# A convolution and two feed-forward layers on one core: other SBUF addresses for the activation tiles, and one gather buffer instead of two

## The chip, the core and the metric

The kernel runs on one core of a Trainium2 chip. The metric is device time in microseconds (us) from the first to the last instruction of one execution. The engines are TensorE (PE; its weight loads are listed apart as PEld), VectorE (DVE), ScalarE (ACT), GpSimd (POOL) and SyncE (SP), whose queue issues nearly all DMAs. SBUF is the on-chip memory of 128 partitions. A tile lies at one byte address, the same in each of its partitions; PSUM is the memory that TensorE writes.

## What is computed

A dynamic convolution with 7 taps and softmax weights over 2 x 4096 tokens of width 192, then two feed-forward layers of width 2048, the first with a leaky ReLU, the second with an ELU.

```python
w = np.exp(weight_gen - max); w = w / (sum(w) + 1e-09)      # per token, head, 7 taps
out = np.einsum('bshk,bskhg->bshg', w, x_unf)               # x_unf: the 7 last tokens
h = x @ w_in;  g = np.maximum(0.01 * h, h);            x = g @ w_out
h = x @ w_in;  g = np.where(h > 0, h, exp(min(h, 0)) - 1);  out = g @ w_out
```

## The kernel before

The 8192 tokens are cut into 16 blocks of 512. Each block goes through layer 0 and layer 1; a layer has 8 units, each of 256 of the 2048 hidden columns, so there are 256 units in all. Blocks 0 and 1 of layer 0 run interleaved at the start, then the two layers take turns: (0, 2), (1, 0), (1, 1), (0, 3), (1, 2), and so on.

All matrices are split into a high and a low part of type float32r, and three of the four partial products are added up. The weights (`win`, `wout`) stay in SBUF. TensorE is used as two halves of 64 rows: `issue` (L830) emits one matmul for the rows 0 to 63 and one for the rows 64 to 127 in turn. Both of a pair stream 512 columns. In the steady state a round of unit s holds 19 such pairs: nine h matmuls of unit s for each half, and ten output matmuls of unit s-4 for each half. The lower half does its h matmuls first, the upper half its output matmuls first; so of the 19 pairs 18 hold one h matmul (moving operand `xt` or `yt`, stationary operand `win`) and one output matmul (moving `gh` or `gl`, stationary `wout`), and one pair holds two output matmuls.

After a round ACT makes `w` from the PSUM tile `h` (L752 or L755, in layer 1 also L759 and, on DVE, L763), then the high part `gh` (ACT, L769) and DVE the low part `gl` (L772). `gh` and `gl` have four buffers each, 4096 bytes per partition.

From block 2 on the input of layer 0 is made by `conv_block` on DVE, transposed in 32 x 32 squares, written to DRAM (`spread`, L551) and read back in another order by two `gather` steps into two `dup` tiles: `gather(0)` is one DMA (L556), `gather(1)` two (L559). `high(0)` and `high(1)` on ACT (L573) and `low(0)` and `low(1)` on DVE (L576) turn them into the one `xt` tile. The first matmul of the block's first round waits for all of these (`fresh` and `tasks` in the code).

A planner (`Plan.order`) sets the order of the instructions on all engines from costs written in the code, the keys and the number of buffers of each ring. With one buffer in a ring, a step that takes it is put behind the last user of the tile before. Tiles are placed in SBUF one after another in the order of their creation: `ident`, `spare`, the weights, and then the rings. `new` (L186) hands a ring's tile out.

Of the kernel before, what the change touches and what calls it, by code (L numbers as in the profile page):

```python
# [8 lines left out]
F32 = mybir.dt.float32  # L9
# [11 lines left out]
P = 128  # L21
# [10 lines left out]
N = BS * P  # L32
# [30 lines left out]
WARM = 14  # L63

FILL = 0.5

HEAD = 30.0

# [97 lines left out]
def conv_moe_kernel(ctx: ExitStack, tc: tile.TileContext, x, wg, wi0, wi1, wo, out):  # L166
# [5 lines left out]
        "xt": (1, [P, 4, N], F32R), "yt": (2, [P, 4, N], F32R),  # L172
        "h": (2, [P, 2, N], F32), "w": (3, [P, 2 * N], F32),
        "gh": (4, [P, 2 * N], F32R), "gl": (4, [P, 2 * N], F32R),
        "dup": (2, [P, N], F32), "c": (1, [P, N], F32), "o": (1, [P, N], F32),
        "raw": (4, [P, 2 * 512 + 2], I32), "t": (2, [P, 512], I32),
    }
    const = ctx.enter_context(tc.tile_pool(name="const", bufs=1))
# [10 lines left out]
    def new(slot):  # L189
        bufs, shape, dt = rings[slot.ring]  # L190
        if slot.ring == "xs":

            if slot.ring not in lasting:
                lasting["xs"] = (sb.tile([P, 2 * shape[1], D], dt, name="xs"), [0])
            tile, n = lasting["xs"]
            r = n[0] % 2 * shape[1]
            slot.tile = tile[:, r : r + shape[1], :]
            n[0] += 1
            return slot.tile
        if bufs == 1 or slot.ring in ("h", "t"):  # L200

            tiles, n = lasting.setdefault(slot.ring, ([], [0]))
            if len(tiles) < bufs:
                pool = {"h": ps, "st": small, "e": small}.get(slot.ring, sb)
                tiles.append(pool.tile(shape, dt, name=f"{slot.ring}{len(tiles)}"))
            slot.tile = tiles[n[0] % bufs]
            n[0] += 1
            return slot.tile
        pool = small if slot.ring in ("ws", "raw") else sb
        slot.tile = pool.tile(shape, slot.dtype or dt, tag=slot.ring, name=slot.ring, bufs=bufs)  # L210
        return slot.tile

    ident = const.tile([P, P], F32, name="ident")
    spare = const.tile([P, 1], F32, name="spare")
    win = {}
    wout = {}
    for l in range(2):
# [29 lines left out]
    def split(src, hi_out, lo_out, key, names):  # L247
# [19 lines left out]
        def load():  # L267
            nc.sync.dma_start(new(raw).bitcast(U16)[:, 1 : 4 * n + 1], src.bitcast(U16))  # L268
# [5 lines left out]
        def leading():  # L274
            middle, top = parts()
            d = new(t)[:, :n].bitcast(F16).rearrange("p (n t) -> p n t", t=2)
            nc.scalar.activation(d[:, :, 1], top, AF.Copy)  # L277
# [51 lines left out]
    def conv_block(i, due):  # L329
# [8 lines left out]
        def load_w():  # L338
            n = BS * H * K
            dst = new(ws).rearrange("p a k -> p (a k)")  # L340
            nc.sync.dma_start(dst, wg[:, i * n : (i + 1) * n])  # L341
# [615 lines left out]
    with tc.manual_schedule():  # L957
# [8 lines left out]
        def turn(bank, count):  # L966
            for n in range(count):
                nc.tensor.matmul(bank[:, N // 2 : N // 2 + P], plain, plain, start=True, stop=True)  # L968
# [9 lines left out]
        for t in order:  # L978
            t.ins = t.emit()
            if t is plan.read_once:  # L980
                spare_bank = acc[1][0]
            turn(spare_bank, int(FILL * gaps.get(t, 0.0) / 0.27))

# [43 lines left out]
```

## Time and profile before

| what | value |
|---|---|
| median of 2 timed runs | 1130.34 us (1129.93 to 1130.75) |
| the profiled execution | 1129.36 us, of which the trace spans 1127.5 us |
| PE busy | 1120.0 us, 99% of the span, 9936 matmul records |
| DVE busy | 782.2 us, 69% |
| ACT busy | 788.5 us, 70% |
| granted TensorE clock | 1.0 in all 40 slices |
| chain that ended last | PE 98% |

The trace can be read by groups of equal instructions, by tile, in order of time and by stretches of time. Durations are of one profiled execution. The ends of matmuls are modelled and overlap with the next start, so the pace of TensorE is read from starts.

### The profile page before, as it was taken

How to read it: one execution, taken by the hardware profiler on the slowest of the kernel's cores; microseconds unless marked ns; L12 is line 12 of the kernel's file. 1: busy time of each engine (PE TensorE's matmuls, PEld its weight loads, DVE VectorE, ACT ScalarE, POOL GpSimd, SP SyncE). 2: the span in 40 equal slices, each digit the busy share in tenths (PEclk: the TensorE clock that was granted, in tenths of full speed). 3: DMA queues.
4: the chain of work that ended last, by engine and by line, in shares of the span. 5: the costliest groups of instructions: out<-in, count | busy, mean ns of one | idle time of the engine just before them, and what ended most of it. 6: DMA issues, size and time to landing. Idle time of an engine off the chain costs nothing.

```text
span 1127.5 us, 23936 instructions
## 1 busy us (share of the span) xinstructions
PE 1120.0 (99%) x9936; PEld 924.7 (82%) x9936; DVE 782.2 (69%) x969; ACT 788.5 (70%) x1011; POOL 11.7 (1%) x19
## 2 busy tenths in 40 slices
PE   8999999999999999999999999999999999999998
PEld 7888888888888888888888888888888888888886
DVE  7877989889899898998974463544636445363565
ACT  7989987575766757658576585756757566575675
POOL 4000000000000000000000000000000000000000
PEclk9999999999999999999999999999999999999999
DMA  6453120222203122030110000000010000000001
GB/s 222 142 159 94 44 73 15 87 73 68 73 1 99 43 68 73 17 122 3 29 34 16 20 1 15 20 16 20 1 34 1 15 20 1 15 1 15 1 1 29
DMA packets 28812, 50.23 MB, mean 45 GB/s; under 512 B 3104, under 2 KB 16288, under 8 KB 28704
## 3 DMA queue, kind: packets, MB, share of 16 engines
q1 hardware_dynamic: 28560, 48.57, 13.9%
q8 instruction: 78, 1.28, 0.5%
q14 instruction: 30, 0.25, 0.1%
q10 hardware_dynamic: 144, 0.13, 0.0%
HBM read 36.90 MB, written 11.80 MB: 43 GB/s over the span
## 4 chain that ended last, share of the span: by engine, by line
PE 98%; DMA 1%; DVE 0%; SPq 0%; issue 0%; ACT 0%; DVEq 0%
PE acc L830 51%; PE h L830 46%; DMA raw<-wi_in 1%; DVE gl L471 0%; PE h L489 0%; SPq L352 0%; DVE yt L457 0%; SPq L341 0%; SPq L268 0%; PE acc L968 0%; ACT raw L272 0%; DVE o L641 0%; DVE st L372 0%; ACT win L284 0%; DVE acc L387 0%
## 5 line engine op out<-in xcount | busy, mean ns | idle before, releaser
L830 PE MATMUL acc<-gh,wout 64*128 64x512 f32 (+1 forms) x3048 | 973.3, 386 | 0.0
L830 PE MATMUL acc<-gl,wout 64*128 64x512 f32 (+1 forms) x2032 | 784.4, 386 | 0.0
L830 PEld LDWEIGHTS acc<-gh,wout 64*128 64x128 f32 (+1 forms) x3048 | 560.9, 184 | 60.2
L830 PE MATMUL h<-yt,win 64*128 64x512 f32 (+1 forms) x2568 | 606.1, 387 | 0.9 <-ACT yt L453 0.9
L830 PEld LDWEIGHTS h<-yt,win 64*128 64x128 f32 (+1 forms) x2568 | 469.8, 184 | 54.1 <-ACT yt L453 1.1
L830 PE MATMUL h<-xt,win 64*128 64x512 f32 x2016 | 476.7, 386 | 0.0
L772 DVE TENSOR_TENSOR gl<-w,gh 128x1024 fp32r<-128x1024 f32 (+1 forms) x257 | 312.4, 1220 | 168.7 <-ACT gh L769 167.7
L830 PEld LDWEIGHTS acc<-gl,wout 64*128 64x128 f32 (+1 forms) x2032 | 374.0, 184 | 40.6 <-issue 0.4
L830 PEld LDWEIGHTS h<-xt,win 64*128 64x128 f32 x2016 | 371.0, 184 | 39.6
L769 ACT ACTIVATE gh<-w 128x1024 fp32r<-128x1024 f32 (+1 forms) x257 | 267.9, 1049 | 3.0
L752 ACT ACTIVATE w<-h 128x1024 f32<-128x1024 f32 x128 | 131.4, 1027 | 193.2 <-PE h L830 190.8
L763 DVE SCALAR_TENSOR_TENSOR w<-w,h 128x512 f32<-128x512 f32 x256 | 164.4, 684 | 127.6 <-ACT w L759 126.5
L755 ACT ACTIVATE w<-h 128x1024 f32<-128x1024 f32 x129 | 131.5, 1020 | 117.2 <-PE h L830 116.5
L759 ACT ACTIVATE w<-w 128x512 f32<-128x512 f32 x256 | 147.5, 624 | 4.0
L428 DVE TENSOR_TENSOR a<-a,prod 128x768 f32<-128x768 f32 x84 | 80.2, 955 | 1.6
L420 DVE TENSOR_TENSOR prod<-xs,ws 128x768 f32<-128x768 f32 x84 | 80.2, 954 | 1.3
L600 DVE TENSOR_TENSOR c<-acc,c 128x512 f32<-128x512 f32 (+1 forms) x32 | 22.0, 687 | 32.6 <-ACT o L649 26.0
L593 ACT ACTIVATE c<-acc 64x512 f32<-64x512 f32 x32 | 19.1, 595 | 4.6 <-PE acc L830 3.8
L272 ACT ACTIVATE raw<-raw 128x384 int32<-128x384 uint32 (+3 forms) x30 | 17.1, 572 | 5.2 <-DMA raw<-wi_in 5.2
L277 ACT ACTIVATE t<-raw 128x384 f16<-128x384 bf16 (+3 forms) x30 | 19.9, 664 | 0.0
L576 DVE TENSOR_TENSOR xt<-dup,xt 128x512 fp32r<-128x512 f32 x28 | 18.0, 686 | 0.0
L281 DVE CUSTOM_DVE_ANT_0 raw<-raw,t 128x768 uint16<-128x768 uint16 (+1 forms) x26 | 15.4, 606 | 1.7 <-ACT t L277 1.7
(56 smaller groups left out, 238.5 us busy)
## 6 DMA issues: line engine op xcount, KB each, us to landing
xs<-x_in SPq DMA_DIRECT2D x14, 960.0 KB, 5.0
raw<-wo_in SPq DMA_DIRECT2D x16, 384.0 KB, 3.5
scratch<-prod SPq DMA_DIRECT2D x56, 96.0 KB, 3.2
raw<-wi_in SPq DMA_DIRECT2D x10, 512.0 KB, 4.2
out_t<-o SPq DMA_DIRECT2D x15, 256.0 KB, 2.6
dup<-scratch SPq DMA_DIRECT2D x14, 256.0 KB, 3.0
dup<-scratch SPq DMA_DIRECT2D x28, 128.0 KB, 2.9
out_t<-c SPq DMA_DIRECT2D x16, 128.0 KB, 2.5
```

The lines of the kernel that those rows point to most:

```text
L277: nc.scalar.activation(d[:, :, 1], top, AF.Copy)
L420: nc.vector.tensor_tensor(out=prods() if k else sums(), in0=rows_of(k, BS + k).rearrange("p s (h g) -> p (s h) g", g=G), in1=scaled(k).to_ ...
L428: nc.vector.tensor_tensor(out=sums(), in0=sums(), in1=prods(), op=ALU.add)
L593: nc.scalar.activation(new(c)[0:64], B[64:P], AF.Copy)
L600: nc.vector.tensor_tensor(out=c.tile[0:n], in0=B[0:n], in1=c.tile[0:n], op=ALU.add)
L752: nc.scalar.activation(cols(w), flat(), AF.Prelu, alpha=0.01)
L755: nc.scalar.activation(cols(w), flat(), AF.Relu, scale=-1.0)
L759: nc.scalar.activation(c, c, AF.Exp, scale=-1.0)
L763: nc.vector.scalar_tensor_tensor(out=c, in0=c, scalar=1.0, in1=h.tile[:, j, :], op0=ALU.subtract, op1=ALU.max,)
L769: nc.scalar.activation(cols(gh), cols(w), AF.Copy)
L772: return nc.vector.tensor_tensor(out=cols(gl), in0=cols(w), in1=cols(gh).bitcast(F32), op=ALU.subtract).ins
L830: i = nc.tensor.matmul(out_ap, w, x_ap, start=start, stop=stop).ins
```

## The change

Four things: the base of nearly all tiles moves up by 32 bytes, since `spare` grows from 4 to 36 bytes and places are given out in steps of 32; each `gh` and `gl` tile gets 16 more columns (64 bytes) behind the 1024 that are used; the ring `dup` has one buffer; and `spare` is filled over 9 columns instead of 1.

```diff
+SHIFT = 16
...
-        "dup": (2, [P, N], F32), "c": (1, [P, N], F32), "o": (1, [P, N], F32),
+        "dup": (1, [P, N], F32), "c": (1, [P, N], F32), "o": (1, [P, N], F32),
...
         pool = small if slot.ring in ("ws", "raw") else sb
+        n = shape[-1]
+        if slot.ring in ("gh", "gl"):
+            shape = [P, n + SHIFT]
         slot.tile = pool.tile(shape, slot.dtype or dt, tag=slot.ring, name=slot.ring, bufs=bufs)
+        if slot.ring in ("gh", "gl"):
+            slot.tile = slot.tile[:, :n]
         return slot.tile
 
     ident = const.tile([P, P], F32, name="ident")
-    spare = const.tile([P, 1], F32, name="spare")
+    spare = const.tile([P, 9], F32, name="spare")
```

The addresses in the two built programs, modulo 512 bytes:

| tiles | before | change |
|---|---|---|
| `ident` | 128 | 128 |
| `win`, `wout`, `xt`, `yt`, `w`, `dup`, `c`, `o` | 160 | 192 |
| `gl`, four buffers | 160 each | 192, 256, 320, 384 |
| `gh`, four buffers | 160 each | 448, 0, 64, 128 |

The slices that matmuls read of `win`, `wout`, `xt` and `yt` start at multiples of 512 bytes within their tiles, those of `gh` and `gl` at multiples of 1024, so the operands have the remainders of the table. In front of the change every moving and every stationary operand of the 64-row matmuls lies at 160.

The order of TensorE's instructions is the same in both programs, row for row. On SP, ACT and DVE the steps of `gather(1)` move. SP at the first block that goes through `dup` (block 2), before (`raw` are weights on their way in, `dup` the gathered block):

```order
L551 DMA scratch<-prod 32x6x128 x4
L268 DMA raw<-wi_in 128x2048
L556 DMA dup<-scratch 128x512
L559 DMA dup<-scratch 64x512 x2
L268 DMA raw<-wi_in 128x2048
L268 DMA raw<-wo_in 128x1536
```

and with the change:

```order
L558 DMA scratch<-prod 32x6x128 x4
L275 DMA raw<-wi_in 128x2048
L563 DMA dup_1115<-scratch 128x512
L275 DMA raw<-wi_in 128x2048
L275 DMA raw<-wo_in 128x1536
L566 DMA dup_1115<-scratch 64x512 x2
```

The two DMAs of `gather(1)` stand behind one load of `wi` and one of `wo`. ACT at the same place, before (`w<-h` and `gh<-w` are two steps of one unit, the other rows weights):

```order
L272 ACTIVATE raw<-raw 128x512
L573 ACTIVATE xt_1176<-dup 128x512 x2
L752 ACTIVATE w<-h_323 128x1024
L769 ACTIVATE gh<-w 128x1024
L277 ACTIVATE t_96<-raw 128x512
L284 ACTIVATE win_76<-raw 128x512
L272 ACTIVATE raw<-raw 128x512
L752 ACTIVATE w<-h_286 128x1024
```

and with the change:

```order
L279 ACTIVATE raw<-raw 128x512
L580 ACTIVATE xt_1173<-dup_1115 128x512
L284 ACTIVATE t_96<-raw 128x512
L759 ACTIVATE w<-h_323 128x1024
L776 ACTIVATE gh<-w 128x1024
L291 ACTIVATE win_76<-raw 128x512
L291 ACTIVATE win_77<-raw 128x512
L279 ACTIVATE raw<-raw 128x512
L580 ACTIVATE xt_1173<-dup_1115 128x512
L759 ACTIVATE w<-h_286 128x1024
```

`high(1)` is now one unit later than `high(0)`, and the next `w<-h` stands behind it. DVE's `low(1)` moves in the same way, behind the next `gl`. In the later blocks the same pair of steps is torn apart by one or two units.

## Rows read from the trace of the kernel before

**Rows 1.** The page: busy time, TensorE's clock in 40 slices, chain that ended last.

```profile
PE 1120.0 (99%) x9936; PEld 924.7 (82%) x9936; DVE 782.2 (69%) x969; ACT 788.5 (70%) x1011; POOL 11.7 (1%) x19
...
PEclk9999999999999999999999999999999999999999
...
PE 98%; DMA 1%; DVE 0%; SPq 0%; issue 0%; ACT 0%; DVEq 0%
```

**Rows 2.** Groups by shape, PE: xcount | busy us, mean ns | idle before.

```profile
L830 PE MATMUL acc<-gh,wout 64*128 64x512 f32 x3024 | 965.7, 386 | 0.0
L830 PE MATMUL acc<-gl,wout 64*128 64x512 f32 x2016 | 778.3, 386 | 0.0
L830 PE MATMUL h<-yt,win 64*128 64x512 f32 x2544 | 599.7, 386 | 0.0
L830 PE MATMUL h<-xt,win 64*128 64x512 f32 x2016 | 476.7, 386 | 0.0
```

**Rows 3.** Order of time, PE, 500 us: start us, us, instruction, xcount.

```profile
500.15 0.39 PE L830 MATMUL acc<-gl,wout 64*128 64x512 f32 x1
500.16 0.39 PE L830 MATMUL h<-yt,win 64*128 64x512 f32 x1
500.38 0.39 PE L830 MATMUL acc<-gh,wout 64*128 64x512 f32 x1
...
504.46 0.39 PE L830 MATMUL acc<-gl,wout 64*128 64x512 f32 x1
504.46 0.39 PE L830 MATMUL h<-yt,win 64*128 64x512 f32 x1
```

**Rows 4.** Order of time, PE, the last unit: 512 columns, then 256.

```profile
1118.97 0.39 PE L830 MATMUL acc<-gh,wout 128*128 128x512 f32 x1
1119.20 0.39 PE L830 MATMUL acc<-gl,wout 128*128 128x512 f32 x1
...
1122.18 0.28 PE L830 MATMUL h<-gl,wout 128*128 128x256 f32 x1
1122.30 0.40 PE L830 MATMUL h<-gh,wout 128*128 128x256 f32 x2
1122.54 0.28 PE L830 MATMUL h<-gl,wout 128*128 128x256 f32 x1
```

**Rows 5.** Order of time, PE, the warm-up matmuls on `ident`; then by tile: min/median/max ns.

```profile
5.21 1.28 PE L968 MATMUL acc<-ident 128*128 128x128 f32 x10
...
L968 PE MATMUL acc<-ident x42: 271/275/582, 1.4 to 20.8; 128*128 128x128 f32 x42
```

**Rows 6.** Three stretches: length, busy us (x) of each engine, PEclk, DMA.

```profile
100.00:400.00 300.00, 300.00 (x2650) 247.82 (x2648) 269.96 (x343) 220.21 (x288) 0.00 (x0) 1.00 0.20 59
400.00:800.00 400.00, 400.00 (x3532) 330.65 (x3530) 273.02 (x322) 267.76 (x330) 0.00 (x0) 1.00 0.11 32
800.00:1000.00 200.00, 200.00 (x1768) 165.29 (x1766) 95.42 (x108) 132.31 (x162) 0.00 (x0) 1.00 0.04 12
```

**Rows 7.** Order of time, block 2's way into `xt`: SP, ACT, DVE, PE.

```profile
67.77 0.34 SPq L556 DMA_DIRECT2D dup<-scratch  x1
68.16 1.16 SPq L559 DMA_DIRECT2D dup<-scratch  x2
71.14 0.34 SPq L268 DMA_DIRECT2D raw<-wi_in  x1
75.45 0.34 SPq L268 DMA_DIRECT2D raw<-wo_in  x1
...
74.49 1.14 ACT L573 ACTIVATE xt<-dup 128x512 fp32r<-128x512 f32 x2
...
80.07 1.03 ACT L752 ACTIVATE w<-h 128x1024 f32<-128x1024 f32 x1 [0.42 <-PE h L830]
...
75.30 1.28 DVE L576 TENSOR_TENSOR xt<-dup,xt 128x512 fp32r<-128x512 f32 x2
...
79.84 0.39 PE L830 MATMUL h<-xt,win 64*128 64x512 f32 x1
```

**Rows 8.** DMA issues: us to landing, all of the run, then from 60 to 84 us.

```profile
dup<-scratch SPq DMA_DIRECT2D x28, 128.0 KB, 2.9
...
dup<-scratch SPq DMA_DIRECT2D x2, 128.0 KB, 4.2
```

**Rows 9.** By tile, `xt` from 217.9 to 254 us (a later block): min/median/max ns, first and last start.

```profile
L830 PE MATMUL h<-xt,win x9: 386/386/386, 252.2 to 254.0; 64*128 64x512 f32 x9
L573 ACT ACTIVATE xt<-dup x2: 613/615/617, 220.0 to 220.5; 128x512 fp32r<-128x512 f32 x2
L576 DVE TENSOR_TENSOR xt<-dup,xt x2: 684/684/684, 221.3 to 221.9; 128x512 fp32r<-128x512 f32 x2
```

**Rows 10.** Order of time, PE: the last h matmul on `xt` of the block before.

```profile
217.50 0.39 PE L830 MATMUL h<-xt,win 64*128 64x512 f32 x1
217.73 0.39 PE L830 MATMUL h<-yt,win 64*128 64x512 f32 x1
```

## The prediction, made before the changed kernel ran

> **What bounds the kernel now.** I read the page first: TensorE is busy for 99% of the span at the full granted clock, and 98% of the chain that ended last is TensorE [rows 1]. The groups by shape say with what: 9600 matmuls of 64 rows and 512 columns, with no idle time ahead of any group [rows 2]. They come as pairs, one for each half of the rows, so they are 4800 pairs. Since the ends of matmuls are modelled, I take the pace from starts: from 500.15 to 504.46 us there are 19 pairs, 4.31 / 19 = 0.2268 us each [rows 3]. 4800 such pairs make 1088 of the 1127.5 us. The time of this kernel is the pace of a pair, and the rest is the head and the tail.
>
> What is in the pace shows in the last unit, where the same matmul runs on 256 columns. Three of them take 1122.54 - 1122.18 = 0.36 us, so 0.120 us each [rows 4]. The 256 columns between the two sizes cost 0.2268 - 0.120 = 0.107 us, or 0.417 ns a column, which is one column in each cycle of 2.4 GHz. Of a pair's 226.8 ns then 213.3 are columns and some 13.3 ns are a constant that each matmul pays whatever its width. No change of address can touch the columns; if addresses matter, they matter in these 13.3 ns, which are 4800 x 13.3 = 64 us of the kernel.
>
> Does another engine slow TensorE down? The stretches say no: from 100 to 400 us DVE is busy for 270 of 300 us, from 800 to 1000 us for 95 of 200, and the matmuls in each microsecond are 2650 / 300 = 8.83, 3532 / 400 = 8.83 and 1768 / 200 = 8.84 [rows 6]. If DVE and ACT collided with TensorE in SBUF, the pace would follow their load, and it doesn't.
>
> **The addresses.** The change moves operands and adds no instruction to TensorE. It could act in two ways.
>
> First, by the remainders relative to each other. Before, moving and stationary operands all start at the same remainder; with the change the `gh` and `gl` tiles stand at eight. But `xt`, `yt` and `win` move together and keep their common remainder, and in 18 of 19 pairs one of the two matmuls is an h matmul on these. TensorE starts the pairs together (500.15 and 500.16, 500.38, and so on [rows 3]); a faster output matmul waits for its slower partner. Were a common remainder the cause of the whole constant, only the one pair of two output matmuls could gain, 13.3 ns x 252 rounds = 3.4 us at most, and I take nothing of it.
>
> Second, by the absolute address: all operands of the pairs go from 160, which is no multiple of 64, to multiples of 64. The only matmuls of the trace whose operands are at such a multiple already are the warm-up's on `ident` (128, both operands). Ten of them, at full clock, start over 1.28 - 0.275 us, so 9 gaps of 0.1117 us [rows 5]. If this plain float32 form takes two column times for each of its 128 columns, 106.7 ns, its constant is 5.0 ns. So the nearest row with a round address has a smaller constant, but it is another type, another width, and its weights never change. The bounds of this term are: -64 us (the constant goes), -40 us (it goes to the 5.0 ns of the warm-up, 4800 x 8.3 ns), 0, and +64 us (it doubles). I take 0, because the constant is equally there in 64-row pairs and in the 128-row matmuls of the last unit [rows 4] and under all loads, as a cost of the instruction would be, and nothing but that one foreign row connects it with an address.
>
> The Trainium skill, "SBUF — State Buffer", section "Specifications (TRN2)", says that SBUF works in lines of 16 bytes, and its section "SBUF: two separate sides" that TensorE waits for no other engine. Both 160 and 192 are multiples of 16, so by this page the move is worth nothing; the stretches above agree with the second point, and no row here shows the first.
>
> **The two elementwise engines.** If the new addresses slow `gl` or `gh`, DVE has cover: 30 of 300 us idle in its fullest stretch [rows 6], and the units run four rounds ahead. Up to a tenth on all of DVE there costs nothing, and I see no reason for any. The wider `spare` is a setup step of 9 columns: nothing.
>
> **One `dup` buffer.** `gather(1)` must now wait until `low(0)` has read the tile. Before, both halves landed early and `high` and `low` ran back to back: ACT from 74.49, DVE's second `low` over at 75.30 + 1.28 = 76.58, first matmul on this `xt` at 79.84 [rows 7]. That is a slack of 3.26 us, and the new chain uses it up. `low(0)` ends at 75.30 + 0.68 = 75.98. The first of the two DMAs occupies SP for half of 1.16 us, so the second is issued at 76.6; the load of `wo` ahead of both (75.45 + 0.34) is out of the way. It lands after 2.9 us (the median) to 4.2 us (what it took in this busy part of the run) [rows 8]; I take 3.5, since only one weight load stands ahead of it: 80.1. Then `high(1)` with 0.62 and `low(1)` with 0.68, and 0.1 for two hand-overs: 81.5 us. The round's first matmul waits for all of it: 81.5 - 79.84 = **1.7 us** of idle TensorE (1.1 at 2.9 us, 2.4 at 4.2 us). Behind `high(1)` on ACT stands the next `w<-h`, due at 80.07 [rows 7] and then at 80.8; it feeds an output matmul four rounds on, so nobody waits for it.
>
> In later blocks the same chain has room. `xt` has one buffer too, so `high(0)` runs only after the block before has left it: last matmul on it at 217.50 [rows 10], `high(0)` at 220.0, `low(1)` over at 222.6, next use at 252.2 [rows 9], a slack of 29.6 us for some 6 us more. The scratch writes of the next block, which now queue on SP behind the waiting `gather(1)`, are hidden by the same slack. Cost 0.
>
> **The sum.** 0 + 1.7 + 0: the profiled execution would go from 1129.36 to 1131.1 us, and the median, 1 us above it, from 1130.34 to 1132.0. Without address effects: 1130 to 1136.
>
> **Rivals.**
> 1. *Round addresses shorten the constant.* For it speaks the 5.0 ns of the warm-up [rows 5], and that the remaining 13.3 ns have no visible cause; against it the different form of that row. All operands of a pair move, so partners don't hold each other up. At 5.0 ns: 1132 - 40 = 1092 us; at half of 13.3 ns: 1132 - 32 = 1100 us. DVE would be at 270 / 289 of its fullest stretch, still no bound. The Trainium skill, "TensorE: Matmul & The Clock Gate", section "Wait — 56ns, not 53.3ns?", gives a constant of 2.5 ns at 2.4 GHz; no run here shows it for this type, and by it the estimate would be 1132 - 52 = 1080 us.
> 2. *New remainders collide (slower).* If a `gh` or `gl` tile at some remainder against `wout` at 192 costs a second 13.3 ns, each pair with that tile is late: 64 / 8 = 8 us for each of the eight. It is slower by over 2% (22.6 us) from three colliding tiles on: 1132 + 24 = 1156 us. For it: the eight are new; against it: a constant pace so far and no sign of any collision.
> 3. *The single buffer stalls every block.* If SP's queue holds `gather(1)` up in all 14 blocks as in the first, 14 x 1.7 = 24 us, 1154 us; with half the blocks, 1142. Against it the 29.6 us [rows 9].
>
> **How the numbers follow.** Addresses do nothing and the first block waits: 0.70. Shorter constant: 0.22, of which 0.07 around 1100 and the rest lower. New collisions: 0.04. Repeated stalls: 0.04, half of it under 1145. The likeliest case gives 1132 us, with its own range 1130 to 1136. For 8 in 10 the range must take in the half-constant case below and part of the stalls above: 1098 to 1145, which leaves out 0.15 below and some 0.05 above. A measurement of this kernel tells about 2% from no change (1108 to 1153): faster 0.22, same 0.72, slower 0.06.
>
> **What would show it.** The starts at 500 us: 19 pairs in 4.31 us, or with the shorter constant in about 4.15. Around 81 us: idle time of TensorE of 1 to 2.5 us behind DVE's `low(1)`, and none before later blocks on `xt`. Different spacing for pairs on different buffers of `gh` would be rival 2. The prediction is wrong if the spacing of pairs moves at all.

## The result and the profile after

| | before | change |
|---|---|---|
| median | 1130.34 us | 1142.94 us |
| runs | 1129.93, 1130.75 | 1142.82, 1143.07 |
| ratio | | 1.0117 (95% interval 1.0100 to 1.0133) |
| span of the profiled execution | 1127.5 us | 1141.0 us |

The change costs 12.6 us, or 1.2%. That is within 2% and inside the range, but it is not the 1132.0 us forecast: 1.2 to 1.6 us of it are the forecast wait, and the other 11 us are a pace of TensorE that moved, which the prediction held to be the sign that it was wrong. That the time lies inside the range is luck: the upper end stood for stalls of the single buffer, and those did not come.

First the page of the changed kernel (busy time, clock, chain), to be held against [rows 1].

```profile
PE 1133.0 (99%) x9936; PEld 1033.8 (91%) x9936; DVE 781.1 (68%) x969; ACT 789.3 (69%) x1011; POOL 11.7 (1%) x19
...
PEclk9999999999999999999999999999999999999999
...
PE 97%; DMA 1%; DVE 1%; issue 0%; SPq 0%; ACT 0%; DVEq 0%; ACTq 0%
```

TensorE has the same 9936 matmuls, the same clock, and 13 us more. DVE and ACT are as busy as before to about 1 us. So neither more work nor a slower engine beside it explains the time. PEld is busy for 109 us more, but a load of 64 rows takes 184 ns in both traces: busy time counts loads that overlap once, and the loads of the two halves, which ran at the same time before, now lie partly side by side. The stretches of the changed kernel (length, PE busy and number of matmuls, clock, DMA), against [rows 6]:

```profile
100.00:400.00 300.00, 300.00 (x2620) 1.00 0.19 58
400.00:800.00 400.00, 400.00 (x3494) 1.00 0.11 32
800.00:1000.00 200.00, 200.00 (x1749) 1.00 0.05 14
```

Fewer matmuls fit into each stretch: 2620 instead of 2650, 3494 instead of 3532, 1749 instead of 1768, so 1.1% fewer in each, whether DVE is busy for 89% of the stretch or for 48%. The slowdown is even over the run and does not follow the other engines' load.

In order of time the changed kernel looks so (PE; start us, us, instruction):

```profile
500.06 0.39 PE L837 MATMUL h<-yt,win 64*128 64x512 f32 x1
500.06 0.39 PE L837 MATMUL acc<-gl,wout 64*128 64x512 f32 x1
...
506.93 0.39 PE L837 MATMUL h<-yt,win 64*128 64x512 f32 x1
507.12 0.39 PE L837 MATMUL acc<-gh,wout 64*128 64x512 f32 x1
507.16 0.39 PE L837 MATMUL h<-yt,win 64*128 64x512 f32 x1
507.35 0.39 PE L837 MATMUL acc<-gl,wout 64*128 64x512 f32 x1
507.40 0.39 PE L837 MATMUL h<-yt,win 64*128 64x512 f32 x1
```

In [rows 3] the two matmuls of a pair start within 0.01 us of each other, in every pair. Here some still do (500.06) and others are 0.04 to 0.05 us apart (507.12 and 507.16, 507.35 and 507.40): the halves of the array no longer march in step.

The spacing depends on the buffer. I took the starts of all 38 matmuls of each steady round and put them in groups by the remainders of the `gl` and `gh` buffer that the round reads. Before there is one group. Mean time of a round from the two traces, from the first start of either half to the next:

| remainder of gl, gh (all else 160 before, 192 after) | rounds | ns a round |
|---|---|---|
| before: 160, 160 | 249 | 4307 |
| change: 320, 448 | 62 | 4334 |
| change: 192, 64 | 62 | 4356 |
| change: 256, 128 | 63 | 4360 |
| change: 384, 0 | 61 | 4373 |

The mean of the four is 4356 ns, 49 ns more than before. Times 252 rounds of this kind, that is 12.3 us. With the wait of the first gathered block it accounts for the 13.5 us between the spans.

That wait is there too. Around it the changed kernel shows, on SP, ACT, DVE and PE:

```profile
76.48 1.16 SPq L566 DMA_DIRECT2D dup<-scratch  x2
...
74.96 0.62 ACT L580 ACTIVATE xt<-dup 128x512 fp32r<-128x512 f32 x1
...
80.36 0.63 ACT L580 ACTIVATE xt<-dup 128x512 fp32r<-128x512 f32 x1 [0.24 <-DMA dup<-scratch]
...
75.77 0.68 DVE L583 TENSOR_TENSOR xt<-dup,xt 128x512 fp32r<-128x512 f32 x1
...
81.03 0.69 DVE L583 TENSOR_TENSOR xt<-dup,xt 128x512 fp32r<-128x512 f32 x1
...
81.77 0.49 PE L837 MATMUL h<-xt,win 64*128 64x512 f32 x1 [1.17 <-DVE xt L583]
```

and among TensorE's waits it is the only new one:

```profile
PE h L837 <- DVE xt L583: 1.2, 1, 1.2
```

One wait, 1.2 us on the matmuls (1.6 us counted on the weight loads, which start earlier). No later block waits.

### The profile page after: what moved, and what is told of

Same layout as the page of the kernel before. It is cut to its first block, busy times and chain, and to the rows that moved or that the text cites. A ratio compares the mean times of both kernels' runs of the same rounds, so it can differ in the third digit from the quotient of the medians.

```text
span 1141.0 us, 23935 instructions
## 1 busy us (share of the span) xinstructions
PE 1133.0 (99%) x9936; PEld 1033.8 (91%) x9936; DVE 781.1 (68%) x969; ACT 789.3 (69%) x1011; POOL 11.7 (1%) x19
## 4 chain that ended last, share of the span: by engine, by line
PE 97%; DMA 1%; DVE 1%; issue 0%; SPq 0%; ACT 0%; DVEq 0%; ACTq 0%
PE acc L837 51%; PE h L837 46%; DMA raw<-wi_in 1%; DMA dup<-scratch 0%; DVE gl L478 0%; PE h L496 0%; DVE xt L583 0%; SPq L359 0%; DVE yt L464 0%; ACT gh L776 0%; ACT w L759 0%; SPq L275 0%; SPq L348 0%; ACT xt L580 0%; PE acc L975 0%
## 5 line engine op out<-in xcount | busy, mean ns | idle before, releaser
L435 DVE TENSOR_TENSOR a<-a,prod 128x768 f32<-128x768 f32 x84 | 80.1, 954 | 1.3
L427 DVE TENSOR_TENSOR prod<-xs,ws 128x768 f32<-128x768 f32 x84 | 80.1, 953 | 1.2
L580 ACT ACTIVATE xt<-dup 128x512 fp32r<-128x512 f32 x28 | 17.4, 623 | 11.6 <-DMA dup<-scratch 11.6
L600 ACT ACTIVATE c<-acc 64x512 f32<-64x512 f32 x32 | 19.1, 596 | 4.7 <-PE acc L837 3.9
```

What stands on the lines that cost most here:

```text
L427: nc.vector.tensor_tensor(out=prods() if k else sums(), in0=rows_of(k, BS + k).rearrange("p s (h g) -> p (s h) g", g=G), in1=scaled(k).to_ ...
L435: nc.vector.tensor_tensor(out=sums(), in0=sums(), in1=prods(), op=ALU.add)
```

## The experiments

The theories: **A**, the distances between the remainders of the operands slow TensorE; **B**, the absolute move from 160 to 192 does; **C**, a round address shortens a matmul's constant. After the first set, A was split into **A1**, the distance of the moving operand from the stationary one counts, and **A2**, any difference between buffers counts.

### The 32 bytes alone

From the change:

```diff
-SHIFT = 16
+SHIFT = 0
...
-        "dup": (1, [P, N], F32), "c": (1, [P, N], F32), "o": (1, [P, N], F32),
+        "dup": (2, [P, N], F32), "c": (1, [P, N], F32), "o": (1, [P, N], F32),
```

> One part of the change alone: every tile moved up by 32 bytes (remainder 192 instead of 160), no extra columns, two dup buffers. Theory A (the remainders of gh and gl against each other and against the weights slow TensorE): all remainders are equal again, so 19 pairs in 4.31 us and 1130 us as before. Theory B (the absolute move off 160 slows it): 4.36 us a round and about 1141 us. Theory C (a round address shortens the constant): under 1100 us.

1129.89 us against 1129.78 us, ratio 0.9999 (0.9989 to 1.0008). Its steady rounds take 4307 ns. The absolute address, which took most of the prediction's doubt, does nothing: B and C fall.

### One gather buffer alone

Before, with one `dup` buffer:

```diff
-        "dup": (2, [P, N], F32), "c": (1, [P, N], F32), "o": (1, [P, N], F32),
+        "dup": (1, [P, N], F32), "c": (1, [P, N], F32), "o": (1, [P, N], F32),
```

> One part alone: one dup buffer, all addresses as before but for the tiles behind dup. All theories: only the first gather block waits, 1.2 to 1.6 us, so 1131 to 1132 us with the pace of pairs at 4.31 us a round. If the single buffer carried more of the 12.6 us than that, it would show here as more than 1133 us.

1131.32 us, ratio 1.0015 (1.0006 to 1.0025): 1.5 us, and rounds of 4307.5 ns. The forecast term was 1.7 us.

### The eight remainders without the 32 bytes

The change, with the old `spare`:

```diff
-    spare = const.tile([P, 9], F32, name="spare")
+    spare = const.tile([P, 1], F32, name="spare")
```

> The change without its 32-byte move: gh and gl at eight remainders (160, 224, 288, 352, 416, 480, 32, 96), the rest at 160, one dup buffer. Theory A: the differences between remainders are those of the change, so the same rounds of 4.33 to 4.37 us by buffer and about 1143 us. Theory B: back to 4.31 us and about 1132 us.

1143.03 us, ratio 1.0117 (1.0100 to 1.0134), the ratio of the change itself. The columns behind the tiles are the cause: 1143.03 - 1131.32 = 11.7 us. Whatever is common to all remainders drops out.

### Matmuls alone, one distance at a time

A kernel that only loads two tiles and runs matmuls of 512 columns on 128 rows, 28 in a row for each arrangement, and pairs of 64-row halves. The layers are left out. `p` and `w` are the two remainders in bytes:

```python
nc.tensor.matmul(bank, wts[r, w // 4 : w // 4 + P], mov[r, p // 4 : p // 4 + N], start=first, stop=last)
```

> Matmuls alone, 28 in a row for each arrangement, no other engine at work; the layers are left out and zeros are stored. Moving and stationary operand at given remainders modulo 512: 128-row stream with moving at d and weights at 0, both at b, pairs of 64-row halves with both at d or one of them, and moving alternating between 0 and d. Theory A: 0.2267 us for equal remainders whatever b, and longer for some d; which of the kinds gets longer says what collides (moving against weights: the constant-d rows; successive moving operands: only the alternating rows). Theory B: the spacing depends on b. If no row gets longer, the slowdown needs the other engines.

Five arrangements in order of time, each row being 16 matmuls (PE; start us, us from the first start to the last end, xcount): moving operand 32, 64, 128 and 256 bytes from the stationary one, then both at 32.

```profile
19.73 3.89 PE L63 MATMUL lo<-mov,wts 128*128 128x512 f32 x16
...
26.22 3.83 PE L63 MATMUL lo<-mov,wts 128*128 128x512 f32 x16
...
39.21 3.90 PE L63 MATMUL lo<-mov,wts 128*128 128x512 f32 x16
...
65.32 3.79 PE L63 MATMUL lo<-mov,wts 128*128 128x512 f32 x16
...
123.72 3.79 PE L63 MATMUL lo<-mov,wts 128*128 128x512 f32 x16
```

Taking off the last matmul's 0.39 us (its end is modelled, so this is rough) and dividing by 15 gaps: 0.2333, 0.2293, 0.2340, 0.2267 and 0.2267 us. From the starts themselves (mean of the last 16 gaps, ns; the 0 is from the stretch with both operands at 0, since the first stretch of the run still holds its slow start):

| distance, bytes | 0 | 32 | 64 | 96 | 128 | 160 | 192 | 224 | 256 |
|---|---|---|---|---|---|---|---|---|---|
| ns a matmul | 226.7 | 233.3 | 229.1 | 233.1 | 233.3 | 234.1 | 233.3 | 233.3 | 226.7 |

From 256 to 480 the row repeats to 0.1 ns. With both operands at the same remainder, all 16 remainders give 226.6 to 226.7 ns. Pairs with both halves at the same distance give the same numbers as the 128-row stream. So with no other engine at work and all matmuls of a stretch alike, the distance modulo 256 sets the pace, and not the address. Where the moving operand alternates between distance 0 and d, the mean is again above 226.7 (229.9 to 233.3 ns) except at 0, 192, 256 and 448. It is not the mean of the two distances: 0 and 192 in turn take 226.7 ns, where 192 alone takes 233.3. So the order counts too.

Pairs whose halves have different distances do not wait for each other at first. With one half at 0 and the other at 32, 64, 96 and then 128, the first keeps its 226.7 ns and the other takes the 229.1 to 233.3 of its own distance, and its lag adds up from arrangement to arrangement to 0.59 us. Only from a lag of about 0.7 us on, with the other half at 160 and more, does the half at 0 slow down too (to 233 ns beside one at 192).

### Steps of 256 bytes in the whole kernel

From the change:

```diff
-SHIFT = 16
+SHIFT = 64
```

> The change with 64 more columns (256 bytes) instead of 16 behind each gh and gl tile: their remainders are 192, 448, 192, 448. Theory A1 (what counts is the distance of the moving operand from the stationary one modulo 256, as the matmuls alone showed 0.2267 us at 0 and at 256): rounds of 4.31 us as before and only the wait of the first block, so 1131 to 1132 us. Theory A2 (any difference between the buffers slows TensorE): rounds of 4.33 us or more, over 1137 us.

1131.27 us, ratio 1.0014 (1.0005 to 1.0024), which is the one-buffer kernel's time. The rounds on buffers at 192 and at 448 take 4308 and 4307 ns. Different buffers, no loss: A2 falls as it was put. Modulo 256 these buffers are alike, so what differences modulo 256 do is not tested here.

### All `gh` and `gl` operands 128 bytes further

The buffers of the run before; the operands start 32 columns into them, so they are alike modulo 256 and 128 bytes from `wout`.

```diff
-            slot.tile = slot.tile[:, :n]
+            slot.tile = slot.tile[:, 32 : 32 + n]
```

> The same buffers, but the operands start 128 bytes into them: gh and gl all at 320 or 64, so all alike modulo 256, and 128 bytes from wout. Theory A1: the output matmuls take 0.2333 us as alone; if a half's slow matmuls only delay that half, a round has 10 x 0.2333 + 9 x 0.2267 = 4.37 us and the kernel 1148 us, if both halves wait for each other 4.43 us and 1163 us. Theory A2 (differences between gh and gl or between buffers): there are none modulo 256, so 1131 to 1132 us.

1150.44 us, ratio 1.0195 (1.0169 to 1.0220). No difference between buffers modulo 256, and 19.1 us over the one-buffer kernel: the distance from the stationary operand costs by itself, as A1 has it. Over 252 rounds that is 76 ns a round, where the estimate with each half delayed only by its own matmuls was 66 ns (1148 us) and the one with both in step 126 ns. The profiled execution was the longest of four (1155.8 us; the others 1149.9 to 1150.6), and its rounds take 4403 ns in the mean. The trace shows a step: up to 153 us they take 4380 ns; then one half takes 27 ns more in each round until it starts 0.23 us behind the other, and from there on both take 4407 ns. An estimate with 4380 ns throughout is 1131.3 + 252 x 0.073 = 1149.7 us, near the other three. What sets off the slower rounds stays open.

```profile
100.00:400.00 300.00, 300.00 (x2595) 1.00 0.20 58
```

This is its first stretch: 2595 matmuls where the change has 2620 and before 2650.

### Can an arrangement be faster than before?

Matmuls alone, 128 rows: fine distances, operands that go on by d and e bytes from matmul to matmul, narrower weights, fewer columns, bfloat16. The layers are left out.

> Matmuls alone again, 128 rows, 28 in a row each; the layers are left out and zeros are stored. Moving operand at fine distances of 4 to 60 bytes; moving operand going on by d and weights by e from each matmul to the next; 96, 64 or 32 weight columns; 384 or 256 moving columns; and bfloat16. If the 13.3 ns over the columns come from a collision of the weight load with the stream, fewer weight columns shrink them, and some pair of d and e may be under 0.2267 us. If they are a fixed cost of a float32r matmul, no arrangement is faster. For bfloat16 either theory allows any distance to be free if it reads half the bytes.

Of the 64 pairs of steps d and e from 0 to 224 bytes only the one with d = e = 0 gives 226.7 ns; the others give 228.4 to 235.1. In seven of them d and e are equal but not 0, so that a matmul's own two operands always lie at the same remainder, and still they take 228.4 to 234.2 ns: equal remainders within a matmul are not enough where they change from one matmul to the next. Fine distances give 226.7 at 28 and at 60 bytes, 228.8 at 12, and up to 240.0 at 20. No arrangement of 512 columns in float32r is under 226.6. Weights of 96, 64 and 32 columns at distance 0 are no faster but slower (229.9, 229.7, 231.7 ns), although the weight loads themselves shorten from 189 to 161, 134 and 108 ns. 384 columns take 173.3 ns and 256 take 120.0, so at distance 0 the 13.3 ns over the columns stay whatever the width. At distance 96 they take 176.6 and 119.9 ns: the loss is 6.4 ns with 512 columns, 3.3 with 384 and none with 256. bfloat16 at distances 0, 32, 64, 96 and 128 is spaced by 215 or 216 ns, but for two gaps of 432 ns, where a record is missing. So the 13.3 ns of the kernel before are a floor of the float32r matmul in all that was tried, and the kernel before, with all remainders equal, stood on it. No version that beats it came out of this, and none was made.

### The rounds of the kernel, matmuls alone

The two halves' operands in the order of a round, with the change's four pairs of remainders in turn for 24 rounds, then 8 rounds all equal, then 8 with `gh` and `gl` 128 bytes off. The layers are left out.

> The matmuls of 40 rounds alone, with the kernel's order of operands in both halves and nothing else at work; the layers are left out and zeros are stored. First 24 rounds with the change's four pairs of remainders in turn, then 8 with all at 192, then 8 with gh and gl 128 bytes off. Theory A1 (the operands' remainders alone): the rounds of the whole kernel come back within 10 ns, by (gl, gh): (192, 64) 4356, (256, 128) 4360, (320, 448) 4334, (384, 0) 4373 ns, all equal 4307 ns, 128 off 4400 ns. If ACT and DVE, which write these tiles, have a share, the uneven rounds are shorter here, down to 4307 ns without them.

| gl, gh | alone, ns a round | in the kernel |
|---|---|---|
| 320, 448 | 4334 | 4334 |
| 192, 64 | 4353 | 4356 |
| 256, 128 | 4380 | 4360 |
| 384, 0 | 4353 | 4373 |
| mean of the four | 4355.0 | 4355.8 |
| all equal | 4307 | 4307 |
| 128 off | 4380 | 4380 up to 153 us, later 4407 |

The mean comes back to 1 ns with ACT and DVE idle, so they have no share in it. Two single rounds are off by 20 ns in opposite directions, which is a miss of the 10 ns expected. The trace of the changed kernel shows why, if each half is timed by itself (tiles and order tell the halves apart). The upper half, which does its output matmuls first, takes 4335, 4353, 4381 and 4353 ns for the four rows of the table, and that is the rounds alone to 1 ns. The lower half takes 4335, 4356, 4358 and 4374. An h matmul has distance 0, but the first six behind output matmuls are still uneven: behind those at 256 and 128 they follow at 224, 231, 236, 228, 232 and 231 ns, and at 227 from there on. The lower half does its output matmuls last, so for it these six count to the next round.

How much of this is distance? From the table of single distances a round would be longer by four times the cost of `gl`'s and six times that of `gh`'s. That estimate gives 26, 40, 49 and 41 ns for the four rows, 39 in the mean. Alone they are 27, 46, 73 and 46 ns longer than the equal ones, 48 in the mean. So the distances account for about four fifths; the rest must lie in the order in which different distances follow one another, and no run here prices that.

## Why the prediction was right and where it was wrong

**The bound: right.** TensorE's pace sets the time, and other engines don't. The 13.5 us between the two spans are the pace (12.3 us) and one wait (1.2 us).

**The single buffer: right, a little long.** Forecast 1.7 us (1.1 to 2.4) with the landing at 80.1, the last `low` over at 81.5. In the trace `high(1)` started with the landing at 80.36, `low(1)` ended at 81.72, and the matmul started at 81.77. The pair before started at 80.20, so this one was due at 80.43 and came 1.3 us late, of which the profile counts 1.2 us as idle; the kernel with that edit alone is 1.5 us longer. That the end of the chain was forecast to 0.2 us is in part luck. The chain began 0.5 us later than in [rows 7] (`low(0)` at 75.77 instead of 75.30), since some twelve rounds with slower pairs lay behind it, which also moved TensorE's due start by 0.6 us; against that, the DMAs landed after 3.1 to 3.3 us and not 3.5. Later blocks did not wait, as the slack of 29.6 us said, so rival 3 did not come.

**The absolute address: right with the value taken.** 0 of -64 to +64 us; the 32 bytes alone changed nothing (0.9999). Rival 1 was priced from the warm-up's 5.0 ns, a row of another type, and matmuls alone show why that row misled: in float32r the constant is 13.3 ns at every one of 16 remainders. The 2.5 ns that the Trainium skill gives in "TensorE: Matmul & The Clock Gate", section "Wait — 56ns, not 53.3ns?", are there for bfloat16 (215.8 ns for 512 columns, 2.5 over 213.3), and not for float32r.

**The relative remainders: the step that failed.** The prediction asked of them only whether they could gain ("Were a common remainder the cause of the whole constant, only the one pair of two output matmuls could gain") and took nothing. That they could lose stood as rival 2, at 0.04, with "no sign of any collision" against it. But the trace of before holds one single distance, zero. A constant pace at one point of a curve says nothing of the curve, and no distance measured here is below that point. In place of the 0 that the prediction took, the eight remainders cost 1143.03 - 1131.32 = 11.7 us, because the pairs slow from 4307 to 4356 ns a round. The right reading of [rows 3] was: this pace is known for equal remainders and for nothing else, so the change leaves the known point in 7 of its 8 tiles, with bounds on both sides.

**Only the constant can change: not borne out.** "No change of address can touch the columns; if addresses matter, they matter in these 13.3 ns" was argued and not read from a row. At distance 96 the loss is none with 256 columns, 3.3 ns with 384 and 6.4 ns with 512. So it goes with the number of columns, at least there, and is not the second constant of rival 2.

**The size of rival 2.** It priced a collision at another 13.3 ns for each pair with a bad tile, 8 us for each of the eight. Measured alone, a distance other than 0 or 256 costs 2.4 to 7.4 ns a matmul, so about half of that at most. All tiles but the one at distance 0 and the one at 256 collide, and the change came to 49 ns in a round of 19 pairs, 2.6 ns a pair. At 8 us each, six colliding tiles would have cost 48 us; they cost 11.7.

**The halves in step: wrong.** That "a faster output matmul waits for its slower partner" was said for a gain. For a loss it would have meant that each slow output matmul delays its pair, in both parts of a round: 126 ns at 128 bytes. Measured were 76, near the 66 of each half paying for its own ten. In [rows 3] the halves start together because both take the same time. With unequal distances the matmuls alone show the faster half keeping its pace until the other is some 0.7 us behind; the rows at 507 us show the halves 0.05 us apart.

**Lines and other engines.** The Trainium skill, "SBUF — State Buffer", section "Specifications (TRN2)", has lines of 16 bytes. All distances in the table of matmuls alone are multiples of 32, so lines of 16 bytes by themselves do not tell them apart. The measurement does (226.7 to 234.1 ns), and it decides here. The section "SBUF: two separate sides" of the same page of the Trainium skill says that TensorE never waits for another engine at its way into SBUF. The traces agree: the four uneven rounds have the same mean, 4355 and 4356 ns, with ACT and DVE idle and with them at work.

## What to carry to other kernels

Where TensorE is the bound and runs float32r matmuls of 512 columns, each with a new stationary operand, keep the starts of moving and stationary operands equal modulo 256 bytes, within a matmul and from one matmul to the next; tiles whose sizes are multiples of 256 do that by themselves. Here 64 bytes behind each tile cost 1%, and operands 128 bytes off cost 2%. And a pace that is constant in a trace is known only for the arrangement that the trace holds: before calling an address neutral, run the matmuls alone over a few distances, which takes one short kernel.

## What was not expected of the hardware

- The spacing of float32r matmuls with a new stationary operand each depends on the distance between their operands in SBUF, with a period of 256 bytes: 226.7 ns at 0, 229.1 at 64, 233 to 234 at the other multiples of 32. It is not a matter of steps of 32 only: 12 bytes give 228.8, 20 give 240.0 and 28 give 226.7. The order of distances counts too: 0 and 192 in turn give 226.7 ns, and operands that step on together by 32 bytes give 234.2.
- At a distance of 96 bytes the loss is 6.4 ns with 512 columns, 3.3 with 384 and none with 256.
- bfloat16 at the five distances tried shows none of this (215 or 216 ns).
- Two halves of 64 rows start in step when all distances are equal. When they aren't, each half keeps its own pace; with matmuls alone only a lag of about 0.7 us slows the faster one. In the whole kernel with its operands 128 bytes off the lag stopped at 0.23 us; why there was not tried.
- Fewer weight columns do not shorten the 13.3 ns that a float32r matmul takes over its columns, and cost 3 to 5 ns where 128 columns are at the minimum.

Why the distance matters, whether by the weight load's reads meeting the stream's, was not isolated: the table shows that the addresses of the two operands count together, and not where they meet.
